# Attention products in order of tiling mode, and row-tiled fp32 scores in every chunk

## The chip, the cores and the metric

The kernel runs on one core of one Trainium2 chip. The metric is the device time of one execution in microseconds (us); lower is better. Instructions run on five engines: TensorE (PE, its weight loads shown as PEld), VectorE (DVE), ScalarE (ACT), GpSimd (POOL) and SyncE (SP), which issues the DMAs here.

## The reference

A gated linear attention over 4 batches, 8 heads, 768 positions and head size 48 feeds two products:

```python
for t in range(S):
    state = alpha[:, :, t, :, None] * state + einsum('bhd,bhe->bhde', k[:, :, t], v[:, :, t])
    y[:, :, t] = einsum('bhd,bhde->bhe', q[:, :, t], state)
x = y.transpose(0, 2, 1, 3).reshape(B * S, H * D)      # 3072 x 384
x = (x @ w_a) * (x @ w_b) @ w_out                      # inner size 1536
h = x @ w_in                                           # inner size 2048
out = (h * cos(h)) @ w_out2
```

## The kernel before

**Attention by chunks.** The positions are cut into 24 chunks of 128, six to a batch. In a chunk q and k are scaled by running products of alpha (`att_pre`), so that the recurrence becomes plain products. The eight heads lie in four pairs p; a pair's two heads are at partitions 0 to 47 (j = 0) and 64 to 111 (j = 1). Per chunk c TensorE does:

- the scores, `att_a`, into two PSUM tiles pa: k against q, 128 x 128 for each head. Up to chunk 8 (`CR`) these are fp32 products of 48 rows, in which j = 0 uses the upper half of the array's rows and j = 1 the lower half (row tiles); chunk 0 goes through the pairs with j inside, chunks 1 to 8 do all of j = 0 and then all of j = 1. From chunk 9 on `att_r` splits k and q into a high and a low fp32r part (ScalarE casts, GpSimd subtracts; q in a block form with zeros, so that one product covers a pair's two heads), and `mm3` takes three full-array passes of 256 columns for each pair. The tiles kr and qr for this are made and zeroed in `att_zero`.
- the transposes of k (pt, L274), except in a batch's last chunk;
- `att_d`: the state's growth pd, column-tiled (the two heads of a pair write different halves of the output partitions), except in a batch's last chunk;
- `att_y`: the output py. For each pair a state product (L340, full width, from the block-diagonal state sbd; none in a batch's first chunk) and then two column-tiled ones (L344) that add the masked scores times v. Chunks 2 and 3 have a wider form of it (L331, L332, L335).

An fp32 product is issued as two passes, which the profile counts as two instructions.

VectorE masks the scores (L284), adds pd to the state (L318), scales it (L292, ScalarE copies it into sbd, L298), and evacuates py into xg together with ScalarE (L358 to L361). These follow in each engine's queue in the order in which the program issues them: `att_b` issues `att_d`, then `att_y`, then `att_x`.

**The two products** run in steps. 72 steps of the first (6 groups of 512 tokens, 12 steps each) are followed by 96 of the second. Each operand is split into high and low fp32r parts, and `mm3` makes three passes of 512 columns for each 128 x 128 block of weights. A step of the first product is 18 such passes into pa and pb (`s1`, the same name pa as the scores' tiles) and 9 into po (`s2`, two steps behind). During the steps of group g the four chunks of group g + 1 are worked in: scores at the end of one step, `att_b` at the end of the next, so between pb and po in TensorE's stream. The scores stand at steps 0, 3, 6 and 8 of a group, in the first group at 2, 4, 6 and 8. Chunks 0 to 3 come ahead of the steps, in the order of the list `START`. During the first group the weights of the first product are decoded, on VectorE above all.

The order on each engine is the program's order. Five PSUM slots (`ps`) are handed on in turn to pa, pb, the score tiles, pt, pd and py, so what is allocated fifth after a tile waits for that tile's last reader. `att_b` allocates pd ahead of py.

Of the kernel before, what the change touches and what calls it, by code (L numbers as in the profile page):

```python
# [6 lines left out]
F32 = mybir.dt.float32  # L7
BF16 = mybir.dt.bfloat16
F32R = mybir.dt.float32r
# [3 lines left out]
ALU = mybir.AluOpType  # L13
# [5 lines left out]
B, H, S, D = 4, 8, 768, 48  # L19
NP = H // 2  # L20
PR = 112
C = 128
# [6 lines left out]
NF1 = FF1 // P  # L29
NF2 = FF2 // P  # L30
KT = DM // P
# [5 lines left out]
ORDER2 = "scywrbnamdp"  # L37
POS0 = (2, 4, 6, 8)
LOV = 3
CR = 8  # L40
ND = 2
START = 'A0 P1 M0 w5 D0 A1 P2 Y0 M1 X0 D1 r4 x0 w6 A2 P3 M2 Y1 X1 s3 b3 r3 D2 n3 s2 a2 A3 M3 Y2 b2 n2 h2 d2 Y3 X2 r2 x1 s1 X3 b1 a1 n1 h1 L0 l1 r1 D3'
SPARE = 6
# [11 lines left out]
def tile_kernel(ctx, tc, al, qk, vt, vz, wts, mask, qr, vr, out):  # L55
    nc = tc.nc
    pool = lambda name, bufs, **kw: ctx.enter_context(tc.tile_pool(name=name, bufs=bufs, **kw))
    const = pool("const", 1)
    wpool = pool("w", 3 * NF1 + SPARE)
# [11 lines left out]
    sbd = [const.tile([PR, NP, PR], F32, name=f"sbd{i}") for i in range(2)]  # L71
# [5 lines left out]
    sb3 = [wpool.tile([PR, KT, P], F32, name=f"sb3{i}", tag="w") for i in range(2)]  # L77
# [10 lines left out]
    x1d = dram.tile([B * NP, PR, S], F32, name="x1d")  # L88
    x2d = dram.tile([P, KT, NT], F32, name="x2d")

# [1 line left out]
    wt = {}  # L92

    def raw_w(i, pool_, tag):
# [71 lines left out]
    def mm3(o, whi, wlo, xhi, xlo, start, stop):  # L166
        nc.tensor.matmul(o, wlo, xhi, start=start, stop=False)  # L167
        nc.tensor.matmul(o, whi, xlo, start=False, stop=False)  # L168
        nc.tensor.matmul(o, whi, xhi, start=False, stop=stop)  # L169

# [1 line left out]
    xg = {}  # L172
    chunk_pos = {}
    c0 = 0
# [4 lines left out]
    st = {}  # L179
# [22 lines left out]
    def att_pre(c):  # L202
        s = st[c]
        a, q, k = s["al"], s["q"], s["k"]
        g = als[c] = s["g"] = att_tile(c, [PR, NP, C + 1], "g")
        rf = att.tile([PR, NP, 1], F32, name=f"rf{c}", tag="rf")
        f = att_tile(c, [PR, NP, C], "f")
        e = nc.vector if c >= n0 else nc.gpsimd

        def kscan(ps_):  # L210
            for p in range(ps_.start, ps_.stop):
                nc.vector.tensor_tensor_scan(out=g[:, p, ::-1], data0=a[:, p, ::-1], data1=floor,
                                             initial=1.0, op0=ALU.mult, op1=ALU.max)
            nc.vector.reciprocal(out=rf[:, ps_], in_=g[:, ps_, 0:1])
            e.tensor_tensor(out=k[:, ps_], in0=k[:, ps_], in1=g[:, ps_, 1:], op=ALU.mult)

        def qscan(ps_):
            for p in range(ps_.start, ps_.stop):
                nc.vector.tensor_tensor_scan(out=f[:, p, :], data0=a[:, p, :C], data1=floor[:, :C],
                                             initial=rf[:, p, :], op0=ALU.mult, op1=ALU.max)  # L220
            e.tensor_tensor(out=q[:, ps_], in0=q[:, ps_], in1=f[:, ps_], op=ALU.mult)

        if c == 0:
            for p in range(NP):
                kscan(slice(p, p + 1))
                qscan(slice(p, p + 1))
        else:
            kscan(slice(0, NP))
            if c - 1 in state:
                att_t(c)  # L230
            qscan(slice(0, NP))
        if c > CR:
            att_r(c)

    kr, qr_ = [], []

    def att_zero():
        for i in range(2):
            kr.append(wpool.tile([PR, NP, C], F32R, name=f"kr{i}", tag="w"))
            qr_.append([wpool.tile([PR, 2, 2, C], F32R, name=f"qr{i}_{h}", tag="w") for h in range(2)])  # L240
            for t in qr_[i]:
                nc.gpsimd.memset(t.bitcast(F32), 0.0)

    def att_r(c):
        s = st[c]
        k, q = s["k"], s["q"]
        nc.scalar.copy(kr[0], k)
        nc.gpsimd.tensor_tensor(out=kr[1], in0=k, in1=kr[0].bitcast(F32), op=ALU.subtract)
        for h in range(2):
            for j in range(2):  # L250
                r = slice(64 * j, 64 * j + D)
                src = q[r, 2 * h:2 * h + 2, :]
                hi, lo = (qr_[i][h][r, :, j, :] for i in range(2))
                nc.scalar.copy(hi, src)
                nc.gpsimd.tensor_tensor(out=lo, in0=src, in1=hi.bitcast(F32), op=ALU.subtract)

    def att_chk(c):
        nc.scalar.activation(junk, als.pop(c), AF.Relu, bias=lim[:PR, 0:1], scale=-1.0, accum_out=stats[:PR, 0, c:c + 1])
# [1 line left out]
    def att_a(c):  # L260
        s = st[c]
        pa = s["pa"] = [ps.tile([P, NP, C], F32, name=f"pa{c}_{j}", tag="ps") for j in range(2)]
        if c > CR:
            for p in range(NP):
                o = pa[p // 2].rearrange("p (a b) c -> p a (b c)", b=2)[:, p % 2, :]
                x = [qr_[i][p // 2][:, p % 2].rearrange("p a b -> p (a b)") for i in range(2)]
                mm3(o, kr[0][:, p, :], kr[1][:, p, :], x[0], x[1], True, True)
        for p, j in [] if c > CR else [(p, j) for p in range(NP) for j in range(2)] if c == 0 else [(p, j) for j in range(2) for p in range(NP)]:
            nc.tensor.matmul(pa[j][:, p, :], s["k"][64 * j:64 * j + D, p, :],
                             s["q"][64 * j:64 * j + D, p, :], start=True, stop=True)  # L270
        if c % CPB != CPB - 1:
            pt = ps.tile([P, NP, PR], F32, name=f"pt{c}", tag="ps")
            for p in range(NP):
                nc.tensor.transpose(pt[:, p, :], s["k"][:, p, :], ident[:PR, :PR])  # L274
            kt = att_tile(c, [C, NP, PR], "kt")
            nc.scalar.copy(kt, pt)
            s["kt"] = kt
# [45 lines left out]
    def att_y(c):  # L323
        s = st[c]
        v = s["v"]
        first = c % CPB == 0
        if ND <= c < n0:
            py = s["py"] = ps.tile([P, KT, C], F32, name=f"py{c}", tag="ps")
            for k in range(KT):
                if not first:  # L330
                    nc.tensor.matmul(py[:, k, :], sb3[c % 2][:, k, :], s["q"][:, KT, :], start=True, stop=False)  # L331
                    nc.tensor.matmul(py[:PR, k, :], sbd[c % 2][:, k, :], s["q"][:, k, :], start=False, stop=False)  # L332
                for i in range(2):
                    for j in range(2):
                        nc.tensor.matmul(py[64 * j:64 * j + 64, k, :], v[:, k, j, i, :], s["a"][j][:, KT if i else k, :], start=first and i == 0, stop=i == 1)  # L335
            return
        py = s["py"] = ps.tile([PR, NP, C], F32, name=f"py{c}", tag="ps")
        for p in (KT, *range(KT)):
            if not first:
                nc.tensor.matmul(py[:, p, :], sbd[c % 2][:, p, :], s["q"][:, p, :], start=True, stop=False)  # L340
            for j in range(2):
                h = 2 * p + j
                m = 64 if j == 0 else D
                nc.tensor.matmul(py[64 * j:64 * j + m, p, :], v[:, h * D:h * D + m],  # L344
                                 s["a"][p // 2][:, 2 * (p % 2) + j, :] if c > CR else s["a"][j][:, p, :], start=first, stop=True)

    def att_x(c):
        py = st[c].pop("py")
# [21 lines left out]
                                  in_=x3.bitcast(F32)[64 * j + 16 * k:64 * j + 16 * k + 16, :, :])  # L370

    def att_b(c, n):
        att_d(c)
        att_y(c)
        at(x_at, n, att_3, *att_x(c))
        del st[c]

# [1 line left out]
    abt = {}  # L379

    def s1(g, f, T):
# [44 lines left out]
            nc.scalar.copy(xo[:, :T], po1[o][:, :T])  # L426
            nc.sync.dma_start(out=x2d[:, o, t0:t0 + T], in_=xo[:, :T])

# [1 line left out]
    x2t = {}  # L430
    x2s = {}

# [68 lines left out]
            nc.scalar.copy(xo, po2[o])  # L501
            nc.sync.dma_start(out=out[o * P:(o + 1) * P, g * G2:(g + 1) * G2], in_=xo)

# [1 line left out]
    ones = const.tile([P, 1], F32, name="ones")  # L505
    nc.gpsimd.memset(ones, 1.0)
    okc = const.tile([P, 2], F32, name="okc")
# [10 lines left out]
        nc.tensor.matmul(pf, okc[:, 1:2], ones, start=True, stop=True)  # L518
        nc.vector.tensor_copy(flag_i, pf)

# [1 line left out]
    def gtile(nm, shape, dt=F32):  # L522
        return wpool.tile(shape, dt, name=nm, tag="w")

# [68 lines left out]
                    nc.scalar.copy(yo, pq[o])  # L593
                    nc.sync.dma_start(out=out[o * P:(o + 1) * P, bass.ds(b * S + hf * HS, HS)], in_=yo)

# [1 line left out]
    W2 = 3 * NF1  # L597
    sched = tc.manual_schedule()
    sched.__enter__()
    steps = [(1, g, f) for g in range(len(GROUPS)) for f in range(NF1)]  # L600
# [3 lines left out]
    pe_at, pre_at, post_at, r_at, s_at, b_at, n_at, a_at, h_at, l_at, d_at, x_at, ld_at = ({} for _ in range(13))  # L604

    def at(d, n, fn, *a):
        d.setdefault(n, []).append((fn, a))
# [2 lines left out]
        for fn, a in d.pop(n, ()):  # L610
            fn(*a)

    # attention of the next group's chunks, spread over a group's steps
    for g in range(len(GROUPS) - 1):
        m = GROUPS[g + 1]
        for i in range(m):
            c = tok[g + 1] // C + i
# [7 lines left out]
            if c + 2 < NCH:  # L625
                at(post_at, n + 1, att_load, c + 2)

    # weights, in the order of use: the first two batches come before the steps
    seq = [(f - 2, [3 * f, 3 * f + 1] + ([3 * f - 4] if f > 1 else [])) for f in range(NF1)]
    seq += [(NF1 - 2, [3 * NF1 - 4, 3 * NF1 - 1])]  # L630
    w2 = list(range(W2, W2 + 2 * NF2))
# [3 lines left out]
    order = [i for m, bl in seq if m < NF1 for i in bl]  # L635
# [23 lines left out]
            at(l_at, m, dec_l, nc.gpsimd, *bl[:LOV])  # L659
            at(d_at, m + 1, dec_l, nc.vector, *bl[LOV:])  # L660

    at(post_at, NF1, att_zero)
    at(post_at, n1 - 3, x2_load, 0)
    for k in range(KT):
        at(post_at, n1 - 2, x2_split, 0, k)
# [24 lines left out]
    firsts = dict(A=att_a, P=att_pre, M=att_m, D=att_d, Y=att_y)  # L690
    decs = dict(r=r_at, s=s_at, b=b_at, n=n_at, a=a_at, h=h_at, l=l_at, d=d_at)
    x0 = {}
    # the first chunks, one token a stage: A to Y and X, x as above, w keeps the
    # tensor engine busy, L loads, r to l are the stages of a decode (minus its step)
    att_pre(0)
    for t in START.split():
        k, i = t[0], int(t[1:])
# [31 lines left out]
    for n in range(end + LAG):  # L729
        one = n < end and steps[n][0] == 1  # L730
        if n < end:
            _, g, f = steps[n]
# [88 lines left out]
```

## Time and the profile before

| | |
|---|---|
| median of 3 runs | 1024.23 us (1023.8 to 1025.31) |
| span of the profiled execution | 1023.6 us |
| TensorE busy | 991.2 us, 4987 matmul instructions |
| VectorE busy | 669.5 us |
| ScalarE busy | 537.9 us |
| GpSimd busy | 251.8 us |
| the chain that ended last | TensorE 80%, VectorE 11%, ScalarE 4% |

The profiled execution has a span (first to last instruction) and no time of its own; the three runs' times lie 0.2 to 1.7 us above that span. In timeline rows the columns are the start, the time taken, engine, line, operation, output and inputs, shapes and count, and in brackets how long the engine was idle before and what released it. In rows by stretch they are the busy time of each engine, with its count of instructions, the granted clock of TensorE, the DMA engines' share and GB/s.

### The profile page before, as it was taken

What the parts mean: (1) busy time and instruction counts of PE and PEld (TensorE: products, weight loads), DVE (VectorE), ACT (ScalarE), POOL (GpSimd) and SP (SyncE); (2) the same over time, 40 slices, a digit from 0 to 9 for tenths busy, and PEclk for the clock granted to TensorE, in tenths of its full rate; (3) what the DMA queues carried; (4) which work ended last, traced back from release to release, by engine and by line L of the source; (5) the groups of instructions that cost most, each with busy time, mean ns of one, the idle gap of its engine ahead of it and who ended that gap; (6) DMA issues with size and microseconds to landing.
All of it is one profiled execution on the core that took longest, in us unless ns stands there. A gap on an engine that the chain in (4) does not pass through costs nothing.

```text
span 1023.6 us, 13942 instructions
## 1 busy us (share of the span) xinstructions
PE 991.2 (97%) x4987; PEld 801.3 (78%) x4987; DVE 669.5 (65%) x1128; ACT 537.9 (53%) x1079; POOL 251.8 (25%) x259
## 2 busy tenths in 40 slices
PE   8879889999999999999999999999999999999996
PEld 5757667888888888787888887888888888888884
DVE  7999995444546355645525999876666666666663
ACT  2766544433433333524326667866666666666653
POOL 4575653111111111312103775410101001010000
PEclk9989779999999999999999999999999999999998
DMA  9725310311121021102013643001010010100000
GB/s 296 240 106 163 100 39 5 102 42 44 39 80 48 22 88 48 47 6 88 21 56 139 184 125 125 0 1 62 1 62 1 1 62 0 62 1 1 32 1 34
DMA packets 36800, 65.81 MB, mean 64 GB/s; under 512 B 5616, under 2 KB 12784, under 8 KB 36720
## 3 DMA queue, kind: packets, MB, share of 16 engines
q1 hardware_dynamic: 36720, 64.82, 20.1%
q8 instruction: 41, 0.67, 0.3%
q14 instruction: 39, 0.32, 0.1%
HBM read 53.19 MB, written 9.44 MB: 61 GB/s over the span
## 4 chain that ended last, share of the span: by engine, by line
PE 80%; DVE 11%; ACT 4%; DMA 2%; issue 2%; POOL 1%; SPq 0%; DVEq 0%; POOLq 0%; ACTq 0%
PE pq L168 6%; PE pq L169 6%; PE pq L167 6%; PE ph L168 6%; PE ph L169 6%; PE ph L167 6%; PE pa L167 5%; PE pa L168 5%; PE pa L169 5%; PE po L167 5%; PE po L169 4%; PE po L168 4%; PE pb L167 4%; PE pb L168 4%; PE pb L169 4%; PE py L344 3%
## 5 line engine op out<-in xcount | busy, mean ns | idle before, releaser
L401 DVE TENSOR_TENSOR asb<-pb,asb 128x512 f32<-128x512 f32 x72 | 49.6, 690 | 166.8 <-PE pb L169 125.0
L168 PE MATMUL pq<-g,w 128*128 128x512 f32 x288 | 112.8, 392 | 1.8 <-DVE g L483 1.6
L167 PE MATMUL pq<-g,w 128*128 128x512 f32 x288 | 112.2, 390 | 0.0
L167 PE MATMUL ph<-x,w 128*128 128x512 f32 x288 | 112.1, 389 | 0.0
L169 PE MATMUL pq<-g,w 128*128 128x512 f32 x288 | 112.1, 389 | 0.0
L168 PE MATMUL ph<-x,w 128*128 128x512 f32 x288 | 112.0, 389 | 0.0
L169 PE MATMUL ph<-x,w 128*128 128x512 f32 x288 | 112.0, 389 | 0.0
L458 DVE SCALAR_TENSOR_TENSOR r<-r,ph 128x512 f32<-128x512 f32 x96 | 66.0, 688 | 66.2 <-ACT r L457 65.7
L456 ACT ACTIVATE r<-r 128x512 f32<-128x512 f32 x96 | 60.7, 632 | 83.6 <-DVE r L452 83.6
L403 ACT CAST ab<-asb 128x512 fp32r<-128x512 f32 x72 | 44.7, 622 | 109.2 <-DVE asb L401 109.1
L451 DVE SCALAR_TENSOR_TENSOR r<-n,ph 128x512 f32<-128x512 int32 x96 | 65.8, 686 | 47.7 <-ACT n L449 47.5
L164 POOL TENSOR_TENSOR w<-w,w 128x384 fp32r<-128x384 f32 x66 | 81.5, 1255 | 51.4 <-ACT w L160 50.6
L167 PE MATMUL po<-ab,w 128*128 128x512 f32 x216 | 90.7, 420 | 0.0
L128 POOL TENSOR_TENSOR w<-w 128x384 int32<-128x384 int32 x68 | 65.9, 989 | 86.0 <-DVE w L122 84.3
L168 PE MATMUL po<-ab,w 128*128 128x512 f32 x216 | 86.9, 402 | 0.0
L169 PE MATMUL po<-ab,w 128*128 128x512 f32 x216 | 86.7, 402 | 0.0
L168 PE MATMUL pa<-xg,w 128*128 128x512 f32 x216 | 84.9, 393 | 1.4 <-DVE xg L361 1.4
L167 PE MATMUL pa<-xg,w 128*128 128x512 f32 x216 | 85.2, 394 | 0.9 <-ACT asb L396 0.7
L169 PE MATMUL pa<-xg,w 128*128 128x512 f32 x216 | 85.0, 394 | 0.0
L167 PE MATMUL pb<-xg,w 128*128 128x512 f32 x216 | 84.6, 392 | 0.1
L168 PE MATMUL pb<-xg,w 128*128 128x512 f32 x216 | 84.3, 390 | 0.0
L169 PE MATMUL pb<-xg,w 128*128 128x512 f32 x216 | 84.3, 390 | 0.0
(107 smaller groups left out, 2100.0 us busy)
## 6 DMA issues: line engine op xcount, KB each, us to landing
w<-wts SPq DMA_DIRECT2D x68, 384.0 KB, 5.5
al<-al SPq DMA_DIRECT2D x24, 225.8 KB, 3.1
k<-qk SPq DMA_DIRECT2D x24, 224.0 KB, 3.2
q<-qk SPq DMA_DIRECT2D x24, 224.0 KB, 3.3
x2d<-xo SPq DMA_DIRECT2D x18, 256.0 KB, 2.2
x2f<-x2d SPq DMA_DIRECT2D x18, 256.0 KB, 3.6
out_t<-yo SPq DMA_DIRECT2D x18, 256.0 KB, 2.0
v<-vt SPq DMA_DIRECT2D x22, 192.0 KB, 3.2
```

Source lines behind the costliest of these rows:

```text
L128: nc.gpsimd.tensor_tensor(out=hi32, in0=hi32, in1=lo32, op=ALU.add)
L164: e.tensor_tensor(out=wt[i][:, 1, :], in0=raws.pop(i), in1=wt[i][:, 0, :].bitcast(F32), op=ALU.subtract)
L167: nc.tensor.matmul(o, wlo, xhi, start=start, stop=False)
L168: nc.tensor.matmul(o, whi, xlo, start=False, stop=False)
L169: nc.tensor.matmul(o, whi, xhi, start=False, stop=stop)
L344: nc.tensor.matmul(py[64 * j:64 * j + m, p, :], v[:, h * D:h * D + m], s["a"][p // 2][:, 2 * (p % 2) + j, :] if c > CR else s["a"][j][:, p ...
L401: nc.vector.tensor_tensor(out=a_sb[:, :T], in0=pab[1][:, :T], in1=a_sb[:, :T], op=ALU.mult)
L403: nc.scalar.copy(ab[:, 0, :T], a_sb[:, :T])
L451: nc.vector.scalar_tensor_tensor(out=r, in0=n, scalar=-C1, in1=p, op0=ALU.mult, op1=ALU.add)
L456: nc.scalar.activation(r, r, AF.Sin, scale=0.5)
L458: nc.vector.scalar_tensor_tensor(out=r, in0=r, scalar=1.0, in1=p, op0=ALU.subtract, op1=ALU.mult, reverse0=True)
```

## The change

In `att_y`, all state products of a chunk are issued first, and then all column-tiled products; the first product into the bank alone starts its accumulation. In `att_b`, `att_y` (and the allocation of py) comes ahead of `att_d`. The scores are fp32 row-tiled products in every chunk, with j inside p, so that the two row tiles alternate. `att_r`, `att_zero`, `CR` and the tiles kr and qr go. `START`, and with it the order of chunks 0 to 3, stays. Comments that the diff also alters are left out.

```diff
-CR = 8
...
             qscan(slice(0, NP))
-        if c > CR:
-            att_r(c)
-
-    kr, qr_ = [], []
-
-    def att_zero():
...
-    def att_r(c):
...
     def att_a(c):
         s = st[c]
         pa = s["pa"] = [ps.tile([P, NP, C], F32, name=f"pa{c}_{j}", tag="ps") for j in range(2)]
-        if c > CR:
-            for p in range(NP):
-                o = pa[p // 2].rearrange("p (a b) c -> p a (b c)", b=2)[:, p % 2, :]
-                x = [qr_[i][p // 2][:, p % 2].rearrange("p a b -> p (a b)") for i in range(2)]
-                mm3(o, kr[0][:, p, :], kr[1][:, p, :], x[0], x[1], True, True)
-        for p, j in [] if c > CR else [(p, j) for p in range(NP) for j in range(2)] if c == 0 else [(p, j) for j in range(2) for p in range(NP)]:
-            nc.tensor.matmul(pa[j][:, p, :], s["k"][64 * j:64 * j + D, p, :],
-                             s["q"][64 * j:64 * j + D, p, :], start=True, stop=True)
+        for p in range(NP):
+            for j in range(2):
+                nc.tensor.matmul(pa[j][:, p, :], s["k"][64 * j:64 * j + D, p, :],
+                                 s["q"][64 * j:64 * j + D, p, :], start=True, stop=True)
...
         if ND <= c < n0:
             py = s["py"] = ps.tile([P, KT, C], F32, name=f"py{c}", tag="ps")
+            if not first:
+                for k in range(KT):
+                    nc.tensor.matmul(py[:, k, :], sb3[c % 2][:, k, :], s["q"][:, KT, :], start=k == 0, stop=False)
+                for k in range(KT):
+                    nc.tensor.matmul(py[:PR, k, :], sbd[c % 2][:, k, :], s["q"][:, k, :], start=False, stop=False)
             for k in range(KT):
-                if not first:
-                    nc.tensor.matmul(py[:, k, :], sb3[c % 2][:, k, :], s["q"][:, KT, :], start=True, stop=False)
-                    nc.tensor.matmul(py[:PR, k, :], sbd[c % 2][:, k, :], s["q"][:, k, :], start=False, stop=False)
                 for i in range(2):
                     for j in range(2):
-                        nc.tensor.matmul(..., start=first and i == 0, stop=i == 1)
+                        nc.tensor.matmul(..., start=first and i == 0, stop=i == 1 if first else (k, i) == (KT - 1, 1))
             return
         py = s["py"] = ps.tile([PR, NP, C], F32, name=f"py{c}", tag="ps")
-        for p in (KT, *range(KT)):
-            if not first:
-                nc.tensor.matmul(py[:, p, :], sbd[c % 2][:, p, :], s["q"][:, p, :], start=True, stop=False)
+        order = (KT, *range(KT))
+        if not first:
+            for p in order:
+                nc.tensor.matmul(py[:, p, :], sbd[c % 2][:, p, :], s["q"][:, p, :], start=p == KT, stop=False)
+        for p in order:
             for j in range(2):
...
     def att_b(c, n):
+        att_y(c)
         att_d(c)
-        att_y(c)
         at(x_at, n, att_3, *att_x(c))
...
-    at(post_at, NF1, att_zero)
```

More of the change, by code (lines that the diff above doesn't have):

```diff
@@ L231, in att_pre @@
             qscan(slice(0, NP))
-        if c > CR:
-            att_r(c)
-    kr, qr_ = [], []
-    def att_zero():
[L238 to L242, printed above, removed]
-    def att_r(c):
[L245 to L255, printed above, removed]
     def att_chk(c):
@@ L328, in att_y @@
             py = s["py"] = ps.tile([P, KT, C], F32, name=f"py{c}", tag="ps")
+            if not first:
[3 more added lines that the diff above has]
+                    nc.tensor.matmul(py[:PR, k, :], sbd[c % 2][:, k, :], s["q"][:, k, :], start=False, stop=False)
             for k in range(KT):
-                if not first:
-                    nc.tensor.matmul(py[:, k, :], sb3[c % 2][:, k, :], s["q"][:, KT, :], start=True, stop=False)
-                    nc.tensor.matmul(py[:PR, k, :], sbd[c % 2][:, k, :], s["q"][:, k, :], start=False, stop=False)
                 for i in range(2):
                     for j in range(2):
-                        nc.tensor.matmul(py[64 * j:64 * j + 64, k, :], v[:, k, j, i, :], s["a"][j][:, KT if i else k, :], start=first and i == 0, stop=i == 1)
+                        nc.tensor.matmul(py[64 * j:64 * j + 64, k, :], v[:, k, j, i, :], s["a"][j][:, KT if i else k, :],
+                                         start=first and i == 0, stop=i == 1 if first else (k, i) == (KT - 1, 1))
             return
         py = s["py"] = ps.tile([PR, NP, C], F32, name=f"py{c}", tag="ps")
-        for p in (KT, *range(KT)):
-            if not first:
-                nc.tensor.matmul(py[:, p, :], sbd[c % 2][:, p, :], s["q"][:, p, :], start=True, stop=False)
+        order = (KT, *range(KT))
[3 more added lines that the diff above has]
+        for p in order:
             for j in range(2):
@@ L343, in att_y @@
                 m = 64 if j == 0 else D
-                nc.tensor.matmul(py[64 * j:64 * j + m, p, :], v[:, h * D:h * D + m],
-                                 s["a"][p // 2][:, 2 * (p % 2) + j, :] if c > CR else s["a"][j][:, p, :], start=first, stop=True)
+                nc.tensor.matmul(py[64 * j:64 * j + m, p, :], v[:, h * D:h * D + m], s["a"][j][:, p, :],
+                                 start=first, stop=first or p == order[-1])
     def att_x(c):
```

## The prediction

> **What bounds the kernel now.** I read the page's engine totals first, then the busy time by stretch, then the waits of TensorE and VectorE, and last TensorE's timeline around single chunks.
>
> ```profile
> span 1023.6 us, 13942 instructions
> ...
> PE 991.2 (97%) x4987; PEld 801.3 (78%) x4987; DVE 669.5 (65%) x1128; ACT 537.9 (53%) x1079; POOL 251.8 (25%) x259
> ```
> ```profile
> core 0: us, PE busy (x) PEld busy (x) DVE busy (x) ACT busy (x) POOL busy (x), PEclk, DMA share, GB/s
> 38.00:134.80 96.80, 80.25 (x407) 62.95 (x402) 90.90 (x161) 59.19 (x136) 59.53 (x54) 0.86 0.45 144
> 134.80:617.00 482.20, 482.20 (x2589) 389.42 (x2590) 276.28 (x486) 204.87 (x452) 133.41 (x139) 0.99 0.21 65
> 617.00:1024.00 407.00, 395.98 (x1738) 325.05 (x1736) 271.46 (x414) 258.29 (x446) 40.66 (x36) 0.99 0.08 28
> ```
> The kernel has two halves. Up to about 134.8 us (chunks 0 to 6 and most of chunk 7's scores) VectorE is the bound: 90.90 of 96.80 us busy, while TensorE rests. From 134.8 to 617 TensorE never stops (482.20 of 482.20), so what is taken out of its stream there ends the kernel earlier, one for one. The waits say the same: TensorE after 136 us waits for next to nothing, and VectorE waits for TensorE.
>
> ```profile
> PE pq L168 <- DVE g L483: 1.6, 4, 0.5
> ```
> ```profile
> DVE asb L401 <- PE pb L169: 125.0, 37, 5.2
> ```
> So the sum is made on TensorE for chunks 8 to 23 (in the second stretch), and on VectorE's chain for the rest.
>
> **State products first, then the column-tiled ones.** TensorE's timeline for chunk 9 (columns: start, time taken, line, tiles, shape, count; an fp32 product is two passes, so "x2" is one product):
>
> ```profile
> 198.69 0.39 PE L169 MATMUL pb<-xg,w 128*128 128x512 f32 x1
> 199.01 0.67 PE L313 MATMUL pd<-v,kt 128*64 128x48 f32 x16
> 199.60 0.47 PE L340 MATMUL py<-q,sbd 112*112 112x128 f32 x2
> 200.00 0.43 PE L344 MATMUL py<-a,v 128*64 128x128 f32 x4
> ...
> 202.66 0.50 PE L167 MATMUL po<-ab,w 128*128 128x512 f32 x1
> ```
> From the last pb product to the first po product pass 202.66 - 198.69 = 3.97 us, with a state product and its column-tiled ones in turn four times. Chunk 5 (no pd), chunk 3 (four state passes in a row) and chunk 6 (no state products at all) give the parts:
>
> ```profile
> 94.21 0.39 PE L169 MATMUL pb<-xg,w 128*128 128x512 f32 x1
> 94.44 0.38 PE L340 MATMUL py<-q,sbd 112*112 112x128 f32 x2
> 94.75 0.54 PE L344 MATMUL py<-a,v 128*64 128x128 f32 x4
> ...
> 97.52 0.50 PE L167 MATMUL po<-ab,w 128*128 128x512 f32 x1
> ```
> ```profile
> 30.92 0.40 PE L331 MATMUL py<-q,sb 112*128 112x128 f32 x2
> 31.15 0.38 PE L332 MATMUL py<-q,sbd 112*112 112x128 f32 x2
> 31.46 0.66 PE L335 MATMUL py<-a,v 128*64 128x128 f32 x8
> ```
> ```profile
> 120.45 0.61 PE L313 MATMUL pd<-v,kt 128*64 128x48 f32 x15
> 120.86 0.30 PE L344 MATMUL py<-a,v 128*48 128x128 f32 x1
> ...
> 121.94 0.50 PE L167 MATMUL po<-ab,w 128*128 128x512 f32 x1
> ```
> Call s the step from one state pass to the next and d the stop at a change into column tiles. Two passes: s + d = 94.75 - 94.44 = 0.31. Four passes: 3s + d = 31.46 - 30.92 = 0.54. So s = 0.115 and d = 0.195, and d is paid at nearly every change. Eight state passes in one block cost 7s + d = 1.00. All column-tiled work of a chunk (pd and py) in one block cost 121.94 - 120.45 = 1.49 in chunk 6, where nothing stands between; py alone 121.94 - 120.86 = 1.08. The state block follows pb with no stop, 94.44 - 94.21 = 0.23. After the change a chunk with pd therefore takes 0.23 + 1.00 + 1.49 = 2.72 instead of 3.97: it saves 1.25. One without pd takes 0.23 + 1.00 + 1.08 = 2.31 instead of 97.52 - 94.21 = 3.31: it saves 1.00. In the TensorE-bound stretch, chunks 8, 9, 10, 13 to 16 and 19 to 22 are of the first kind: 11 x 1.25 = 13.75. Chunks 11, 17, 23 are of the second: 3.0. Chunks 12 and 18 start a batch, have no state products, and only swap two column-tiled blocks: 0. Sum 16.75; bounds: one more stop d per chunk (-2.7), or a seamless join (+0.4).
>
> **Moving pd behind py** makes pd end about 2 us later relative to py, and with it VectorE's new state, ScalarE's copies of it and, queued behind them on both engines, the evacuation of py. Nobody on TensorE needs the state before the next chunk, two or three steps on; what becomes late is py's PSUM slot (below).
>
> **Scores.** Chunk 8, still in the fp32 form but one row tile after the other, and chunk 9 in the three-pass form:
>
> ```profile
> 166.22 0.39 PE L169 MATMUL pb<-xg,w 128*128 128x512 f32 x1
> 166.54 1.71 PE L269 MATMUL pa<-q,k 48*128 48x128 f32 x16
> 168.18 0.60 PE L274 MATMUL pt<-ident,k 112*128 112x112 f32 x4
> 168.55 0.48 PE L167 MATMUL po<-ab,w 128*128 128x512 f32 x1
> ```
> ```profile
> 190.68 0.39 PE L169 MATMUL pb<-xg,w 128*128 128x512 f32 x1
> 190.91 0.28 PE L167 MATMUL pa<-qr,kr 112*128 112x256 f32 x1
> ...
> 192.35 0.55 PE L274 MATMUL pt<-ident,k 112*128 112x112 f32 x4
> 192.66 0.48 PE L167 MATMUL po<-ab,w 128*128 128x512 f32 x1
> ```
> Chunk 8's sixteen passes take 168.18 - 166.54 = 1.64, less than the 15s + d = 1.92 of a serial run, so the two tiles already overlap where one half meets the other. Chunk 0 alternates; its last pair, four passes, was this:
>
> ```profile
> 9.80 0.80 PE L269 MATMUL pa<-q,k 48*128 48x128 f32 x4 [0.46 <-POOL q L221]
> ...
> 14.73 3.09 PE L269 MATMUL pa<-q,k 48*128 48x128 f32 x16 [1.11 <-POOL q L221]
> ```
> The second row is chunk 1: the same sixteen passes as chunk 8 in 3.09 instead of 1.71, so the clock is about half there. At half speed four alternating passes took 0.80, twice the 0.38 of two serial full-speed passes (chunk 5's row): two tiles ran side by side. I take the alternating block as eight passes, 1.00, plus 0.10 for its first: 1.10. Bounds are 1.00 and chunk 8's 1.64. Chunk 8 saves 0.54. For the others, entry, scores and transposes go from 192.66 - 190.68 = 1.98 to 0.32 + 1.10 + 0.37 = 1.79: 12 x 0.19 = 2.3. Chunks 11, 17, 23 have no transposes and pay about 0.1 on the way back: from 0.23 + 1.44 to 0.32 + 1.10 + 0.1, 3 x 0.15 = 0.45. Sum 3.3.
>
> **Casts and subtractions of att_r, memsets of att_zero.** They go from ScalarE and GpSimd, busy 204.87 and 133.41 of 482.20 us: off the path, 0. They only let py be evacuated earlier.
>
> **Before 134.8 us** TensorE's savings fall into its own idle time, with two exceptions. Chunk 1's alternation is worth twice 0.54 at half clock, and VectorE stood behind it through py of chunk 0:
>
> ```profile
> 21.32 0.29 DVE L359 TENSOR_TENSOR x<-py,x 112x128 fp32r<-112x128 f32 x1 [1.30 <-ACT x L358]
> ```
> Of these 1.30 I take back 1.0 (bounds 0 and 1.3), which VectorE's chain carries to chunk 7. The other is a loss. PSUM slots rotate over five; with py allocated ahead of pd, the second score tile of a chunk that comes two steps after another gets py's slot, where it had pd's. For chunk 7:
>
> ```profile
> 130.36 2.94 PE L269 MATMUL pa<-q,k 48*128 48x128 f32 x16 [2.01 <-DVE asb L401]
> 134.77 0.98 PE L274 MATMUL pt<-ident,k 112*128 112x112 f32 x4 [1.47 <-DVE xg L361]
> ```
> ```profile
> 137.00:140.00 3.00, 3.00 (x9) 0.50 0.22 40
> ...
> 141.00:144.00 3.00, 3.00 (x15) 1.00 0.11 33
> ```
> Now only the transposes wait for xg; after the change nearly all scores do, and alternating stalls both tiles. They start at about 134.7 and push TensorE back by about 2.0 at half clock, 1.0 at full, as the clock comes back at 141 either way: -1.0 (bounds 0 and -2.0). Chunk 7's py block then saves 1.25. Net for the early part 1.0 - 1.0 + 1.25 = 1.25.
>
> The longer wait, from 130.4 to 134.7, could also delay the clock's return; I charge nothing, as the rows have it at 0.50 there already, after waits of 2.01 and 1.47 (rival E has the price). [...]
>
> **Sum.** 16.75 + 3.3 + 1.25 = 21.3. The profiled span of 1023.6 becomes 1002.3. The median of the runs, 1024.23, lies 0.6 above the span, so 1002.9.
>
> **Rivals.** A: alternation overlaps no better than chunk 8's halves at full clock. Then scores cost 0.32 + 1.64 + 0.37 = 2.33 against 1.98, a loss of 0.35 (0.39 without transposes): 16.75 - 5.4 + 0.25 = 11.6 saved, 1012.6. For it: chunk 0 had a gap between its pairs, so no long alternating run is seen. Against: 0.80 for four passes.
> B: the slot of py also holds chunks 11, 15, 19, 23. The tightest is chunk 19:
>
> ```profile
> 418.44 0.56 DVE L361 TENSOR_TENSOR xg<-py,xg 112x384 fp32r<-112x384 f32 x1 [0.65 <-ACT xg L360]
> ```
> ```profile
> 419.38 0.28 PE L167 MATMUL pa<-qr,kr 112*128 112x256 f32 x1
> ```
> The slot came free at 419.0, 0.4 us before the scores, and pd now comes last. Against: VectorE and ScalarE were late there because of att_r's casts, which go. If each of the four waited 1.5 us: 1008.9.
> C: the change brings nothing, since VectorE or ScalarE takes over: 1024. Against: 276.28 and 204.87 busy of 482.20.
> D: slower. Each switch of row tile drains like a mode change: sixteen passes at s + d = 0.31 are 5.0 instead of 1.44 or 1.64, some 3.6 lost x 16 = 57, less 17: about 1064. It decides from a score block of 2.4 us on, where the 17 us are used up. Against: chunk 0's 0.80, which such stops would have made over 1.2. [...]
> E: after the longer wait before chunk 7's scores the clock stays at half for one more stretch like that from 137 to 140. TensorE did half its full-speed work in it, so 3 us cost 1.5: 1004.4. For it: the wait is twice as long. Against: from 137 on TensorE is busy in both kernels.
>
> **Numbers.** Forecast 1002.9 with chance 0.70, A 0.10, B 0.07, C 0.03, D 0.04, E 0.06. Best case of all bounds: 21.3 + 0.4 + 1.6 + 0.3 + 1.0 = 24.6 saved, 999.6. Worst short of A: 21.3 - 2.7 - 1.0 - 1.0 = 16.6, 1007.6. The range 1000 to 1009 takes in B and E. A difference of 0.2% (2 us) is about what a measurement tells. Faster: forecast, A, B and E, 0.93; same, C, 0.03; slower, D, 0.04.
>
> **What would show it.** Chunk 9's stretch from pb to po: 2.7 us with eight state passes 0.115 apart. Score blocks of 1.1 us with both tiles starting together. TensorE without waits after 135 us. Chunk 7's scores released by xg. VectorE's wait at 21.3 us nearly gone. Wrong: score blocks of 1.6 or more; L269 waiting for xg in chunks 11, 15, 19 or 23; or TensorE waiting for VectorE between 150 and 165 us, where VectorE still works off its queue.

## The result and the profile after

| | before | changed |
|---|---|---|
| median | 1024.58 us (1023.8 to 1025.31) | 1002.59 us (1002.12 to 1002.88) |
| ratio, 95% interval | | 0.9785 (0.9771 to 0.9798) |
| span of the profiled execution | 1023.6 us | 1000.4 us |

The change saves 22.0 us in the medians; 21.3 had been forecast. The spans differ by 23.2, because the profiled execution of the kernel before took longer than its median (see "The clock at the start" below). The totals of the page and the stretches that answer to those of before (columns as there):

```profile
span 1000.4 us, 13762 instructions
...
PE 959.0 (96%) x5047; PEld 786.2 (79%) x5047; DVE 647.4 (65%) x1128; ACT 504.9 (50%) x1004; POOL 184.6 (18%) x180
```
```profile
38.00:134.00 96.00, 73.38 (x385) 58.54 (x385) 90.09 (x159) 58.71 (x133) 59.54 (x53) 0.87 0.45 147
134.00:595.00 461.00, 460.42 (x2652) 380.40 (x2652) 254.32 (x487) 172.59 (x378) 66.49 (x61) 0.99 0.23 68
```
TensorE runs 60 instructions more (sixteen passes instead of twelve in 15 chunks) and is busy 32 us less. It is still the bound from 134 us on. To see where the time left, one takes two marks that both kernels have, the first pa pass of step 12 (the first step of group 1) and of step 71 (the last of the first product). TensorE's timeline, before and then changed (the lines of the changed kernel are one lower at this place, more further down):

```profile
162.37 0.39 PE L167 MATMUL pa<-xg,w 128*128 128x512 f32 x1
```
```profile
608.18 0.39 PE L167 MATMUL pa<-xg,w 128*128 128x512 f32 x1
```
```profile
160.72 0.40 PE L166 MATMUL pa<-xg,w 128*128 128x512 f32 x1
```
```profile
585.59 0.39 PE L166 MATMUL pa<-xg,w 128*128 128x512 f32 x1
```
Between the marks pass 445.81 and 424.87 us: 20.94 us were saved in chunks 8 to 23, and 1.65 ahead of them. After step 71 the spans differ by another 0.6, which is no larger than the scatter of that last stretch over the runs below (414.8 to 415.6).

Chunk 9's output products and pd, and its scores, in the changed kernel:

```profile
194.98 0.39 PE L168 MATMUL pb<-xg,w 128*128 128x512 f32 x1
195.20 1.04 PE L315 MATMUL py<-q,sbd 112*112 112x128 f32 x8
196.17 1.09 PE L320 MATMUL py<-a,v 128*64 128x128 f32 x16
197.09 0.62 PE L284 MATMUL pd<-v,kt 128*48 128x48 f32 x16
197.64 0.50 PE L166 MATMUL po<-ab,w 128*128 128x512 f32 x1
```
```profile
187.18 0.39 PE L168 MATMUL pb<-xg,w 128*128 128x512 f32 x1
187.50 1.16 PE L240 MATMUL pa<-q,k 48*128 48x128 f32 x16
188.59 0.60 PE L245 MATMUL pt<-ident,k 112*128 112x112 f32 x4
188.97 0.48 PE L166 MATMUL po<-ab,w 128*128 128x512 f32 x1
```
The state block takes 196.17 - 195.20 = 0.97, the column-tiled work 197.64 - 196.17 = 1.47, the whole from pb to po 2.66 (before: 3.97). The scores take 1.09, and with entry and transposes 1.79 (before: 1.98). Chunk 11, without pd:

```profile
233.70 0.39 PE L168 MATMUL pb<-xg,w 128*128 128x512 f32 x1
...
235.91 0.50 PE L166 MATMUL po<-ab,w 128*128 128x512 f32 x1
```
2.21, where the same chunk took 3.20 before (from 240.40 to 243.60 us), and chunk 5, from which the prediction had worked, 3.31. TensorE's waits after 134 us (who waited for whom: total, times, longest):

```profile
PE pt L245 <- DVE xg L337: 2.3, 1, 2.3
PE pq L167 <- DVE g L459: 1.5, 4, 0.5
PE po L167 <- DVE ab L384: 0.6, 1, 0.6
```
Nothing on the scores (L240) is among them: in no later group do they wait for a PSUM slot. The first row reaches in from chunk 7, the third is at 152 us; both are taken up below.

### The profile page after: what moved, and what is told of

Same layout as the page of the kernel before. It is cut to its first block, busy times and chain, and to the rows that moved or that the text cites. A ratio compares the mean times of both kernels' runs of the same rounds, so it can differ in the third digit from the quotient of the medians.

```text
span 1000.4 us, 13762 instructions
## 1 busy us (share of the span) xinstructions
PE 959.0 (96%) x5047; PEld 786.2 (79%) x5047; DVE 647.4 (65%) x1128; ACT 504.9 (50%) x1004; POOL 184.6 (18%) x180
## 4 chain that ended last, share of the span: by engine, by line
PE 79%; DVE 11%; DMA 4%; ACT 3%; issue 1%; SPq 0%; DVEq 0%; ACTq 0%
PE pq L167 6%; PE pq L168 6%; PE pq L166 6%; PE ph L168 6%; PE ph L167 6%; PE ph L166 6%; PE po L166 5%; PE po L167 4%; PE po L168 4%; PE pa L166 4%; PE pa L167 4%; PE pb L167 4%; PE pb L166 4%; PE pa L168 4%; PE pb L168 4%; DVE w L106 3%
## 5 line engine op out<-in xcount | busy, mean ns | idle before, releaser
L372 ACT COPY asb<-pa 128x512 f32<-128x512 f32 x72 | 42.1, 585 | 119.6 <-PE pa L168 118.8
L166 PE MATMUL pb<-xg,w 128*128 128x512 f32 x216 | 84.1, 389 | 0.1
L167 PE MATMUL pb<-xg,w 128*128 128x512 f32 x216 | 84.0, 389 | 0.0
```

The costliest lines, as they stand in the source:

```text
L372: nc.scalar.copy(a_sb[:, :T], pab[0][:, :T])
```

## The experiments

Each kernel is the changed one with the edit shown, unless said otherwise, and was timed beside the kernel before on the same chip. "Step 12 to 71" is the stretch between the two marks.

**The scores alone.**

```diff
     def att_b(c, n):
-        att_y(c)
         att_d(c)
+        att_y(c)
...                       # att_y: a state product and its column-tiled ones in turn, as before
```


> Only the scores change (alternating fp32 products in all chunks, no casts or subtractions for them); the output products keep the old order, a state product and its column-tiled ones in turn, behind pd. Theory (what counts is TensorE's own stream, block by block): chunk 8 saves 0.54 us, chunks 9 to 23 0.15 to 0.2 each, 3.3 to 3.5 together, and VectorE's early chain 1.0 through chunk 1, so 1024.6 - 4.5 = 1020.1 us (1019 to 1021). Rival (the gain came from relieving ScalarE and GpSimd, whose 15 sets of casts and subtractions go here too): most of the 22 us, 1003 to 1007.

1020.59 us (1019.89 to 1025.52), ratio 0.9971 (0.9957 to 0.9984). Step 12 to 71 takes 442.21, 3.60 less than before. Relief of ScalarE and GpSimd is not where the time came from.

**The output products alone.** The kernel before, with only the new `att_y` and `att_b`.

> Only the order of the output products changes (state products first, then the column-tiled ones, then pd); the scores keep their old forms, with the casts and subtractions. Theory: 11 x 1.31 + 3 x 0.97 = 17.3 us in chunks 8 to 23, and 0.7 to 1.3 in chunk 7, so 1024.6 - 18.4 = 1006.2 us (1005.5 to 1007). Rival (relief of ScalarE and GpSimd): 1017 or more. If the two parts of the change depend on each other, this gain and that of the scores alone do not add up to 22.

1007.06 us (1005.69 to 1007.4), ratio 0.9833 (0.982 to 0.9846), just above the expected range. Step 12 to 71 takes 428.41, 17.40 less than before. With the 3.60 of the scores that makes 21.00, and the whole change has 20.94 there: the two parts add up, and do not lean on each other.

**Scores not alternating.**

```diff
-        for p in range(NP):
-            for j in range(2):
-                nc.tensor.matmul(...)
+        for p, j in [(p, j) for p in range(NP) for j in range(2)] if c == 0 else [(p, j) for j in range(2) for p in range(NP)]:
+            nc.tensor.matmul(...)
```


> The changed kernel, but with the scores of chunks 1 to 23 going through all of j = 0 and then all of j = 1. Theory (two row tiles run side by side only where products of both are next to each other): the score block goes back from 1.09 to 1.64 us, 16 x 0.55 = 8.8 in chunks 8 to 23, and VectorE's early chain loses its 1.0: 1002.6 + 9.8 = 1012.4 us (1011 to 1013.5). Rival (the order within the scores is indifferent, and the gain in them came from dropping the three passes): 1002.6 to 1003.

1012.92 us (1011.96 to 1013.49), ratio 0.9893 (0.9879 to 0.9907). Chunk 9's scores:

```profile
188.71 1.71 PE L239 MATMUL pa<-q,k 48*128 48x128 f32 x16
190.34 0.60 PE L244 MATMUL pt<-ident,k 112*128 112x112 f32 x4
```
The same sixteen passes take 1.63 instead of 1.09, and from step 12 to 71 the kernel loses 8.99 us, 0.56 in each of 16 chunks. That is the price of the order alone. Without alternation the fp32 form is slower than the three-pass form it replaced (rival A's case): step 12 to 71 takes 433.86 here and 428.41 in "The output products alone", which has the new order of the output products and the old scores. So the whole of the scores' part hangs on the order of two loops.

**Output products in two halves.**

```diff
-        if not first:
-            for p in order: ...          # four state products
-        for p in order: ...              # eight column-tiled ones
+        for half in (order[:2], order[2:]):
+            if not first:
+                for p in half: ...
+            for p in half: ...
```


> The changed kernel, but the output products go in two halves: two state products, their column-tiled ones, the other two state products, their column-tiled ones. Theory (each return from column tiles to full width and back costs the same, 0.32 us): one more such return in 14 chunks from 8 on, 4.5 us, chunk 7's partly hidden: 1002.6 + 4.5 = 1007.1 us (1006 to 1008). Rival (it is the one unbroken accumulation into the bank that is fast, and any return loses the whole gain): about 1016. Rival (changes of mode are free and the gain comes from the place of pd): 1002.6.

1007.12 us (1006.71 to 1007.77), ratio 0.9837 (0.9824 to 0.985). Chunk 9:

```profile
195.28 0.60 PE L316 MATMUL py<-q,sbd 112*112 112x128 f32 x4
195.81 0.65 PE L321 MATMUL py<-a,v 128*64 128x128 f32 x8
196.39 0.69 PE L316 MATMUL py<-q,sbd 112*112 112x128 f32 x4
...
198.04 0.50 PE L166 MATMUL po<-ab,w 128*128 128x512 f32 x1
```
One more return to full width costs 198.04 - 195.28 = 2.76 against 2.44, 0.32 a chunk; step 12 to 71 grows by 4.69, 14 x 0.335. The cost is one for each round trip, not for losing an unbroken accumulation.

**pd ahead of py.**

```diff
     def att_b(c, n):
-        att_y(c)
         att_d(c)
+        att_y(c)
```


> The changed kernel, but with pd issued (and allocated) ahead of py again, as in the kernel before. Theory: pd then makes a trip of its own into column tiles and back, 0.33 us in the 11 chunks from 8 on that have pd and state products, 3.6 together, chunk 7's hidden: 1002.6 + 3.6 = 1006.2 us (1005.3 to 1007). Rival (pd late costs something elsewhere, since the new state, its copies and the evacuation of py queue up behind it): less than 3 us, down to a gain.

1006.11 us (1005.35 to 1006.8), ratio 0.9815 (0.9783 to 0.9848). pd makes a trip of its own into column tiles:

```profile
195.16 0.39 PE L168 MATMUL pb<-xg,w 128*128 128x512 f32 x1
195.48 0.67 PE L284 MATMUL pd<-v,kt 128*64 128x48 f32 x16
196.08 1.13 PE L315 MATMUL py<-q,sbd 112*112 112x128 f32 x8
197.13 1.09 PE L320 MATMUL py<-a,v 128*64 128x128 f32 x16
198.15 0.50 PE L166 MATMUL po<-ab,w 128*128 128x512 f32 x1
```
2.99 instead of 2.66; step 12 to 71 grows by 3.59, 11 x 0.33. Of the 1.31 us that a chunk saves, 0.33 come from moving pd and 0.98 from the three inner round trips. That pd is late in the changed kernel costs nothing that shows.

**The casts put back.** `att_zero` and `att_r` as before, with no reader of what they make.

> The changed kernel, with the casts and subtractions of k and q for chunks 9 to 23 and the memsets put back on ScalarE and GpSimd; no product reads what they make. Theory (they lie off the path): 1002.6, within 0.7. Rival (part of the gain came from relieving these engines): 1004 to 1010, with waits of TensorE for ScalarE or VectorE in chunks 9 to 23.

1002.89 us (1002.25 to 1003.26), ratio 0.9787 (0.9773 to 0.9801): as the changed kernel. The casts and subtractions were off the path.

**Chunk 1 not alternating.**

```diff
+        ... [(p, j) for j in range(2) for p in range(NP)] if c == 1 else [(p, j) for p in range(NP) for j in range(2)]
```


> The changed kernel, but chunk 1's scores go through all of j = 0 and then all of j = 1. Theory of the prediction (chunk 1's alternation shortens VectorE's chain by 1.0 us): 1003.6 us. Rival (the clock that the run happens to have at 15 us sets that: at full clock the order is worth 0.55, and parts of it are hidden): 1002.6 to 1003.2, and in the trace chunk 1's sixteen passes take 1.7 at full clock or 3.1 at half.

1003.85 us (1002.52 to 1004.79), ratio 0.9794 (0.9762 to 0.9826). The profiled execution had the full clock at 15 us, by the 1.71 that sixteen such passes also took in chunk 8 of the kernel before, at a granted clock of 1.00:

```profile
14.68 1.71 PE L239 MATMUL pa<-q,k 48*128 48x128 f32 x16 [1.30 <-POOL q L220]
```
The kernel before, in its profile, needed 3.09 for these passes, and the changed one this:

```profile
14.90 2.08 PE L240 MATMUL pa<-q,k 48*128 48x128 f32 x16 [0.47 <-POOL q L220]
```
Of the other traces some have this chunk at half clock and some at full, with no tie to the edit: alternating, the sixteen passes took 2.08 in "The scores alone" and 1.16 in "pd ahead of py". The median is 1.4 us above that of the next kernel, timed in the same series, but the ranges of the two overlap, and the profiled execution has a span of 1000.6 us, level with the 1000.4 of the changed kernel. That chunk 1's alternation is worth about 1 us at the median fits this; it is not shown. What the traces say of this term stands under "The clock at the start" below.

**The transposes' PSUM tile allocated first, then the transposes issued first.** Two attempts to give the second score tile the slot of py, as the prediction had thought the change would.

```diff
     def att_a(c):
+        pt = ps.tile(...)                       # first attempt
+        for p in range(NP):                     # second attempt: these too
+            nc.tensor.transpose(pt[:, p, :], ...)
         pa = s["pa"] = [ps.tile(...) for j in range(2)]
```


> The changed kernel, but the PSUM tile of the transposes is allocated ahead of the two score tiles, so that the second score tile gets the slot of py, as the prediction had thought. Theory: chunk 7's scores, but for the first passes, then wait for xg (until about 133.8 us) and push TensorE back by 1.0 to 2.0 us at the transposes; the wait of po for ab at about 155 us takes up 0.6 of it: 1002.6 + 0.4 to 1.4 = 1003.0 to 1004.0 us, no waits of L240 in chunks 11, 15, 19, 23. Rival (such a wait halves the clock for a further window, or the later chunks wait too): 1005 or more.

1002.45 us (1001.54 to 1003.34), ratio 0.978 (0.9748 to 0.9812), and a trace with the waits of the changed kernel: the edit moved nothing. In the second attempt the first use of the tile moves as well, and with it the waits: in these two kernels a slot was settled at a tile's first use.

> The changed kernel, but the transposes are issued ahead of the scores, so that they take the slot that comes free first and the scores the slots of pd and py. (Where a slot goes is settled at a tile's first use, so that allocating the transposes' tile earlier alone had moved nothing.) Theory: chunk 7's scores, all but the first passes, now wait for xg until about 133.8 us, as the prediction had thought of the change itself; po follows 2.0 us after xg (half clock) instead of 0.7, a loss of 0.7 us at full speed, of which the wait of po for ab at about 155 us takes up most. On TensorE the block of transposes and scores costs up to 0.1 more in each later chunk, up to 1.3. Together 1002.6 to 1004.6 us. Rival (the longer wait keeps the clock at half for a window longer, or the chunks two steps after another wait in later groups too): 1005 or more.

1002.74 us (1002.51 to 1002.83), ratio 0.9787 (0.9773 to 0.9801). Chunk 7:

```profile
129.79 0.48 PE L244 MATMUL pa<-q,k 48*128 48x128 f32 x2 [0.27 <-ACT st L288]
133.24 2.07 PE L244 MATMUL pa<-q,k 48*128 48x128 f32 x14 [2.96 <-DVE xg L338]
135.23 0.79 PE L166 MATMUL po<-ab,w 128*128 128x512 f32 x1
```
Now the scores do wait for xg, and po starts 2.0 us after it, with the clock at half (the po products follow one another at 0.43 us there, at 0.23 in chunk 9), as the prediction had pictured. TensorE reaches step 10 later for it, 14.69 us after xg instead of 13.61. Yet by step 12 nothing of that is left: step 12 starts 26.97 us after xg here and 26.99 in the changed kernel, since TensorE's wait for ab around 152 us is gone in return. In chunks 8 to 23 the new order costs 0.68 us in all (step 12 to 71 takes 425.55), within the 1.3 allowed for it.

**ScalarE's copies of py ahead of pd.** A version that the traces suggested: with py ahead of pd, ScalarE can copy it while VectorE adds the state.

```diff
     def att_b(c, n):
         att_y(c)
-        att_d(c)
-        at(x_at, n, att_3, *att_x(c))
+        at(x_at, n, att_3, *att_x(c, att_d))    # ScalarE's two copies, att_d, VectorE's two subtractions
```


> The changed kernel, but ScalarE's copies of py are issued ahead of pd, and VectorE's subtractions for them after the state: with py ahead of pd, ScalarE can copy py while VectorE adds the state. Theory (up to 134 us VectorE's chain sets the time, and it waits 1.3 + 0.65 us for ScalarE in each of chunks 4 to 7): 1.5 to 1.95 us less in chunks 4, 5, 6 and 7, 4.5 to 7 together: 1002.6 - 5.8 = 996.8 us (995.6 to 998.2). Rival (the waits hide other work of the same chain, or TensorE before 134 us is the bound after all): 1001 to 1003.

998.82 us (998.0 to 1001.62), ratio 0.9748 (0.9715 to 0.9781). VectorE in chunk 4, in the changed kernel and in this one:

```profile
84.49 0.60 DVE L263 TENSOR_TENSOR ts<-st,g 112x192 f32<-112x192 f32 x1
86.38 0.29 DVE L335 TENSOR_TENSOR x<-py,x 112x128 fp32r<-112x128 f32 x1 [1.29 <-ACT x L334]
87.32 0.56 DVE L337 TENSOR_TENSOR xg<-py,xg 112x384 fp32r<-112x384 f32 x1 [0.65 <-ACT xg L336]
```
```profile
83.11 0.28 DVE L339 TENSOR_TENSOR x<-py,x 112x128 fp32r<-112x128 f32 x1
83.31 0.54 DVE L340 TENSOR_TENSOR xg<-py,xg 112x384 fp32r<-112x384 f32 x1
```
Both waits are gone. Chunk 6's xg is done 5.1 us earlier and step 12 starts 5.05 us earlier, inside the expected range; the median gains 3.8, less than the range allowed. In the trace 0.7 of the difference went into the last stretch, which took 415.6 us here and 414.8 in the changed kernel; its cause was not found, and another run below (1004.08 us) has a last stretch of 415.6 too.

**GpSimd takes the multiplications of k and q in chunks 4 to 7** (on top of the last edit).

```diff
-        e = nc.vector if c >= n0 else nc.gpsimd
+        e = nc.vector if c >= 2 * n0 else nc.gpsimd
```


> The kernel with ScalarE's copies of py ahead of pd, and besides GpSimd takes the two multiplications of k and q in chunks 4 to 7 from VectorE. Theory (VectorE's chain is still the bound up to 129 us, 1.35 us of it in each of these chunks): up to 5.4 us less than 998.8, so 994 to 997. Rival (GpSimd takes 1.2 us for each, the scores wait for it, and VectorE slows down beside it, so the chain moves to GpSimd): 998.8 or more.

1004.08 us (1003.67 to 1005.08), ratio 0.9801 (0.9787 to 0.9815): 5.3 us worse than without it. VectorE had less to do, but single instructions of it took much longer while GpSimd worked on the weights beside it (from 80.6 to 89.6 us):

```profile
80.04 2.75 DVE L386 TENSOR_TENSOR ab<-asb,ab 128x512 fp32r<-128x512 f32 x1
...
83.09 3.54 DVE L263 TENSOR_TENSOR ts<-st,g 112x192 f32<-112x192 f32 x1
```
L263 takes 0.60 in the rows above and 3.54 here, L386 2.75 where at its quickest it takes 0.67. The other half of the rival came true as well: from 60 us on TensorE's scores wait 3.0 us for the q that GpSimd now makes, and not at all without the edit. How much of the 5.3 us each of the two costs was not separated.

**VectorE makes the weights' low parts itself** (instead of the last edit).

```diff
-LOV = 3
+LOV = 0
```


> The kernel with ScalarE's copies of py ahead of pd, and besides the weights' low parts in the first group (26 subtractions of 128 x 384, 1.15 us each on GpSimd) are made by VectorE, one step later. Theory 1 (VectorE's chain is the bound and slows down beside GpSimd: its bitwise step L106 takes 1.18 us in the middle of the decode and 0.54 at the least): VectorE gains up to 25 x 0.63 = 16 us and pays 26 x 0.5 to 0.7 = 13 to 18, so 995 to 1001 us, near 998.8. Theory 2 (VectorE's chain is the bound and GpSimd does not slow it; its long instructions are its own): VectorE pays 13 us or more, 1010 or above.

993.88 us (993.11 to 994.7), ratio 0.9704 (0.969 to 0.9717), the fastest of all, and a little below the range. VectorE's groups from 38 to 129 us (line, shapes, count, busy time, mean in ns), in the kernel with the copies ahead and in this one:

```profile
L106 DVE SCALAR_TENSOR_TENSOR w<-w 128x384 uint32<-128x384 uint32 x25 | 25.1, 1056 | 0.0
L218 DVE TENSOR_TENSOR_SCAN f<-al,rf,lim 112x128 f32<-112x128 f32 x16 | 13.1, 875 | 0.0
...
L211 DVE TENSOR_TENSOR_SCAN g<-al,lim 112x129 f32<-112x129 f32 x16 | 10.3, 704 | 0.0
```
```profile
L163 DVE TENSOR_TENSOR w<-w,w 128x384 fp32r<-128x384 f32 x25 | 19.4, 825 | 0.0
L106 DVE SCALAR_TENSOR_TENSOR w<-w 128x384 uint32<-128x384 uint32 x27 | 16.2, 653 | 0.0
...
L218 DVE TENSOR_TENSOR_SCAN f<-al,rf,lim 112x128 f32<-112x128 f32 x16 | 6.4, 463 | 0.0
L211 DVE TENSOR_TENSOR_SCAN g<-al,lim 112x129 f32<-112x129 f32 x16 | 5.5, 399 | 0.0
```
VectorE took on 19.4 us of subtractions and still finished earlier (chunk 6's xg by 5.7 us): its bitwise steps and its two kinds of scans became faster by 0.3 to 0.4 us each, which gave back 8.9 + 6.7 + 4.8 = 20.4 us.

## Why the prediction was right, and where not

- **State products and column-tiled ones in blocks.** Right in kind and size: 2.66 measured for 2.72, 2.21 for 2.31. The output products' order gave 17.40 by itself where the sum had 16.75, a little more than the upper bound of 17.15: both blocks came out shorter than their estimates (0.97 for 1.00 and 1.47 for 1.49). What costs is the round trip, as the sum had it with its stop d: halves and pd-first each bring back one, 0.32 and 0.33 us.
- **Scores.** 1.09 for 1.10, and 3.60 in all for 3.3. Two tiles run side by side at full clock (sixteen alternating passes in 1.09 at a granted clock of 1.00, 1.63 where they do not alternate) as they did at half, which rivals A and D had denied. A round trip into column tiles cost 0.32; the 1.09 hold fifteen changes of row tile.
- **att_r and att_zero at nothing.** Right, shown by putting them back: 1002.89.
- **The slot of py: this step failed.** It said that slots rotate by five, so that the second score tile of a chunk two steps after another gets py's. In the trace of the changed kernel chunk 7 shows otherwise:

```profile
129.46 0.48 PE L240 MATMUL pa<-q,k 48*128 48x128 f32 x2 [2.62 <-DVE asb L377]
130.33 1.16 PE L240 MATMUL pa<-q,k 48*128 48x128 f32 x14 [0.38 <-ACT st L287]
133.78 1.01 PE L245 MATMUL pt<-ident,k 112*128 112x112 f32 x4 [2.29 <-DVE xg L337]
```
The score tile waits for the reader of pd (st), the transposes for that of py (xg), as before the change. So the order in which pd and py are allocated, by which the prediction and the description of the kernel before went, made no difference. The waits fit slots that are handed on in the order in which the old tiles' last readers are issued, where pd still comes ahead of py; no run changes that order by itself. The -1.0 did not occur. Forcing it, with the transposes issued first, showed a second error in the same step: the 1.08 us that it costs TensorE up to step 10 were close to the 1.0, but its price in time is 0, because VectorE's queue still holds TensorE back at 152 us.
- **The early part, 1.25 forecast, 1.65 measured: near by luck.** The pieces were 1.0 from VectorE's chain, -1.0 for the slot, 1.25 from chunk 7's py. Measured: chunk 6's xg is done 0.9 earlier (133.73 for 134.63), and the slot costs 0. Step 10, the first behind chunk 7's py, begins 2.79 us earlier, in the kernel before and then in the changed one:

```profile
150.13 0.39 PE L167 MATMUL pa<-xg,w 128*128 128x512 f32 x1
```
```profile
147.34 0.39 PE L166 MATMUL pa<-xg,w 128*128 128x512 f32 x1
```
From xg to there TensorE needs 13.61 us instead of 15.50, 1.89 less. About 1.3 of that is chunk 7's py, by what a later chunk with pd saves. The rest, about 0.6, fits the clock, which the prediction had back at 141 "either way". The granted clock was 0.56 from 140 to 141 us before, so half until about 140.9, and 0.79 from 138 to 140 in the changed kernel, so half until about 138.8: after xg TensorE spends 5.1 us at half clock instead of 6.3, and 1.2 us at half clock are worth 0.6. Of the 2.79 us, 1.14 are then lost: steps 10 and 11 take 13.38 instead of 12.24. Of this loss 0.58 is the wait for VectorE below; what the rest waits for the trace does not name:

```profile
152.39 0.50 PE L167 MATMUL po<-ab,w 128*128 128x512 f32 x1 [0.58 <-DVE ab L384]
```
That leaves 1.65. The sum had charged a loss that did not come, and had left out a gain from the clock and a loss behind VectorE; the three nearly cancel. It put VectorE's reign to an end at 134.8; its queue reaches to about 152, the very sign of being wrong that the prediction had named for 150 to 165 us.
- **The clock at the start.** The 1.0 rested on one execution, in which chunk 1's passes took 3.09, about half speed by the 1.71 of other executions (that trace's record of the clock begins only at 21.4 us). VectorE then waited 1.30 for py of chunk 0. In the changed kernel, alternating at a granted clock of 0.50 (15 to 17 us), it does not wait (first row); with chunk 1 not alternating but at the full clock, it does not wait either (second row):

```profile
20.32 0.29 DVE L335 TENSOR_TENSOR x<-py,x 112x128 fp32r<-112x128 f32 x1
```
```profile
19.89 0.27 DVE L334 TENSOR_TENSOR x<-py,x 112x128 fp32r<-112x128 f32 x1
```
In these traces, then, the order of chunk 1's scores moves VectorE's chain only where that chunk runs at half speed; at full clock, chunk 6's xg is done at 133.58 both with chunk 1 alternating (pd ahead of py) and without (chunk 1 not alternating). So the 0.9 above belongs to the execution as much as to the change. And that execution of the kernel before was a long one: in its runs beside the experiments the time lies 1.74 to 1.92 above the span, so the span of 1023.6 stands for about 1025.4, 0.8 above the median.
- **Rivals.** B: no wait of the scores in later groups. C: TensorE busy 460.42 of 461.00. E: the stretch at half clock did not grow; it went from about 132.0 to 138.8 us instead of 130.7 to 140.9, and the scores did not wait for xg. With the transposes issued first they did, and by step 12 that cost nothing.

## What to carry to other kernels

Order a matmul stream by the mode of the array: here each trip into column tiles and back cost 0.32 us, whichever products made it, and two row tiles overlapped from end to end only where their products alternated, 1.09 against 1.63 us for the same sixteen passes. Price such a change block by block on the engine that is the bound, and mark where that engine begins to be the bound: behind that mark the forecast held to 5%, ahead of it 1.14 us of a saving on TensorE were lost again, in part behind VectorE's queue, and a forced loss of 1.08 us there cost nothing in the end. Before moving work from a busy VectorE to GpSimd, look at what VectorE's instructions take while GpSimd runs: here the move back to VectorE was the gain (998.82 to 993.88 us), and more work on GpSimd a loss (to 1004.08).

## What the runs showed of the hardware that was not expected

- In the kernel before, the passes of two row tiles overlapped across program order: the first pass of the second tile started ahead of the last passes of the first (in chunk 2 at 22.73 us, where the last of the first tile started at 23.06; the records are told apart by their spacing, 0.11 us from one pass of a tile to its next). This fits the 1.64 that all of j = 0 and then all of j = 1 took, instead of a serial 1.92. The program's order, which the description of the kernel before gives for each engine, is not the order of these starts.
- VectorE beside GpSimd: a scan of 112 x 128 took 0.46 us on average with GpSimd's subtractions for the weights' low parts gone and 0.88 with them, the bitwise step 0.65 and 1.06; with more work on GpSimd one instruction took 3.54 instead of 0.60. The runs show that the longer durations go with GpSimd's work; by what means they do not show.
